# A gated linear attention block with a SiLU feed-forward: the second chunk's scores ahead of the first chunk's y

## The chip, the cores and the metric

The kernel runs on one core of a Trainium2 chip. The metric is the device time of one execution in microseconds (us), the median of a few runs. A core has five engines that work side by side: TensorE (PE in the profile; PEld is its loading of weights), VectorE (DVE), ScalarE (ACT), GpSimd (POOL) and SyncE (SP), which here issues the DMAs of inputs. An engine takes its instructions in the order of its own queue and waits on semaphores for the others.

## The reference

Inputs are q, k, v and alpha of shape (4, 8, 768, 48): batch, heads, tokens, channels. The attention is a recurrence with a decay for each channel; its output, heads side by side, is the input of a feed-forward block.

```python
for t in range(S):
    state = alpha[:, :, t, :, None] * state + np.einsum('bhd,bhe->bhde', k[:, :, t], v[:, :, t])
    y[:, :, t] = np.einsum('bhd,bhde->bhe', q[:, :, t], state)
x = y.transpose(0, 2, 1, 3).reshape(B * S, H * D)   # 3072 x 384
h = x @ w_in                                        # 384 x 2048
out = (h * (1.0 / (1.0 + np.exp(-h)))) @ w_out      # 2048 x 384
```

The weights arrive as 64-bit floats and are rounded to 32 bits on the chip.

## The kernel before

**Chunks.** The 768 tokens are cut into six chunks of 128, for each of four batches: 24 pieces of work, called chunks here and numbered n = 0 to 23; the first four are the first chunks of the four batches. For a chunk the recurrence becomes matrix products: with the running product of alpha, k is multiplied by the decay from its token to the chunk's end, q is divided by the same, and a lower triangle of q times k (the scores) gives what tokens of one chunk do to one another.

**Four stages for each chunk.**

- `products(n)` (L698): TensorE transposes alpha, k and q of the eight heads in four pairs (L717). ScalarE copies alpha (L719), VectorE scans it backwards for the running product u (L722), makes kp = k times u (L733), and by a reciprocal, a second scan (L752) and a product (L758) makes qp.
- `scores(n)` (L780): eight products of kp and qp into two PSUM banks (L793), two copies by ScalarE into the tile g (L800), two selects by GpSimd that put zeros above the diagonal (L801), four transposes of kp (L818) and their copy kn (L820).
- `values(n)` (L831): y from v and g (and, from the second chunk of a batch on, from the state and qp), into one PSUM bank (L846), and a copy into xt (L851), the input of the feed-forward.
- `states(n)` (L852): products of kn and v (L862) that are added to the batch's state, for the first chunk copied (L870).

**Buffers.** g is one tile, `decayed` (L552), for all chunks. kn comes from the pool `work`, with one buffer. The PSUM banks of the attention come from a pool of three (`ps_attn`, L435), handed out in turn; k and q of the first four chunks are transposed into banks of the feed-forward instead. `gpool` (L422) has six large tiles for the feed-forward's activations, 2048 numbers a partition, the first of which is asked for in step 2.

**Order.** A loop (L1185) runs over 25 steps, each with up to four slots. A step has a list of stages with a lag: as a rule the scores of the chunk before, the products of this chunk, then y and the states of the chunk before. In step 1 the products come first. After each slot `fill` (L1166) puts in other work: at first the conversion of w_in, 24 pieces in all with w_out's following (`weights`, L614: a rounding by ScalarE, L629, and three passes by VectorE, L645 to L647), and from step 2 on pieces of the feed-forward, whose TensorE products need xt and w_in. w_in comes in column groups of 512 with three pieces each; two products groups of 256 columns use one column group. The instructions of a stage are then placed by a scheduler, so TensorE's queue isn't exactly the order of the loop: in the kernel before, the third chunk's transposes stand in the middle of the second chunk's y. SyncE's queue is the order of the loads; `fetch` (L513) asks for the next piece of weights when a buffer comes free.

Before the change TensorE's queue at the start reads: transposes of chunks 0 and 1; scores 0; y 0; states 0; scores 1; alpha 2; y 1 with k 2 and q 2 in it; states 1; two groups of products with w_in; scores 2.

Of the kernel before, what the change touches and what calls it, by code (L numbers as in the profile page):

```python
# [8 lines left out]
F32 = mybir.dt.float32  # L9
# [346 lines left out]
def quotients(  # L356
# [38 lines left out]
    C = 128  # L395
    NCH = S // C
    NP = H // 2
# [11 lines left out]
    TB = GB * C // 2  # L409
    HO = HD // 2  # L410

    def pool(name, bufs=1, space=None):
        kw = {} if space is None else {"space": space}
        return ctx.enter_context(tc.tile_pool(name=name, bufs=bufs, **kw))
# [5 lines left out]
    work = pool("work")  # L420
    xtp = pool("xtp", 4)
    gpool = pool("gpool", 6)  # L422
# [12 lines left out]
    def ps_attn(n=C):  # L435
        return ps_a.tile([128, 512], F32, name="ps_a").rearrange("p (j c) -> p j c", c=n)
# [29 lines left out]
    def load(n, names="akq"):  # L466
        if n == NT:
            return
        c = ctxs.setdefault(n, dict(zip(("ci", "b"), divmod(n, B))))
        b, rows = c["b"], slice(c["ci"] * C, c["ci"] * C + C)  # L470
        for name, src in (("a", alpha), ("k", k), ("q", q)):
            if name not in names:
                continue
            x = src[b, :, rows, :]
            if n < NA:
                c[name] = nat[name][n % NIN]
                nc.sync.dma_start(c[name][:, :, 0:D], x.transpose([1, 0, 2]))
                continue

            c[name] = late["quads"][name]
            for u in range(2):
                for i in range(2):
                    r = 64 * u + 32 * i
                    nc.sync.dma_start(
                        c[name][r : r + 32, 32 * (1 - i) :][:, 0 : 4 * NP * D].rearrange(
                            "p (g c) -> p g c", g=NP),
                        x[u::2].rearrange("h (b j) d -> b h (j d)", j=4))
# [6 lines left out]
    def load_v(n):  # L496
        c = ctxs.setdefault(n, dict(zip(("ci", "b"), divmod(n, B))))
        x = v[c["b"], :, c["ci"] * C : c["ci"] * C + C, :].transpose([1, 0, 2])
        t = c["v"] = vns[n % NV]
        if n < NA:  # L500
            nc.sync.dma_start(t[:, :, 0:D], x)
            return
        nc.sync.dma_start(t[:, 0 : H // 2, 0:D], x[:, 0 : H // 2])
        for e in range(2):
            nc.sync.dma_start(t[CH * e : CH * e + CH, H // 2 :, 0:D], x[CH - CH * e : C - CH * e, H // 2 :])
# [46 lines left out]
    decayed = fix.tile([128, 2 * NP * C], F32, name="g")  # L552
# [227 lines left out]
    def scores(n):  # L780
        c = ctxs[n]
        ci, b = c["ci"], c["b"]
        ps = [ps_attn() for _ in range(2)]

        for j in (0, 2, 1, 3):
            for e in range(2 if n >= NA else 1):
                for u in range(2):
                    r = slice(64 * u, 64 * u + D)  # L790
                    at = slice(CH * e, CH * e + CH) if n >= NA else slice(0, C)
                    t = slice(CH * (e ^ j // 2) if n >= NA else 0, C)
                    pe.matmul(ps[u][at, j, t], lhsT=c["kp"][r, j, at], rhs=c["qp"][r, j, t],  # L793
                              start=True, stop=True)
        g = decayed.rearrange("p (u j c) -> p u j c", u=2, j=NP)
        swapped = decayed.rearrange("p (o u j c) -> p o u j c", o=2, u=2, j=NP // 2)
        c["g"] = (lambda u, j: g[:, u, j, :]) if n < NA else (
            lambda u, j: swapped[:, j // 2, u, j % 2, :])
        for u in range(2 if n < NA else 0):
            act.copy(g[:, u], ps[u])  # L800
            gps.affine_select(g[:, u], g[:, u], pattern=[[0, NP], [1, C]], compare_op=ALU.is_ge,  # L801
                              fill=0.0, base=0, channel_multiplier=-1)
        if n >= NA:
            ps = [x.rearrange("p (o j) c -> p o j c", o=2) for x in ps]
            for u in range(2):
                act.copy(swapped[:, :, u, :, CH:], ps[u][:, :, :, CH:])  # L806
            for r, o in earlier:
                for u in range(2):
                    act.copy(swapped[r, o, u, :, 0:CH], ps[u][r, o, :, 0:CH])
            for at, half in ((CH, later), (0, earlier)):  # L810
                for r, o in half:
                    x = swapped[r, o].rearrange("p u j c -> p (u j) c")[:, :, at : at + CH]
                    gps.affine_select(x, x, pattern=[[0, NP], [1, CH]],  # L813
                                      compare_op=ALU.is_ge, fill=0.0, base=0, channel_multiplier=-1)
        if n < NA and ci < NCH - 1:
            ps_k = ps_attn()
            for j in range(NP):
                pe.transpose(ps_k[:, j, :], c["kp"][:, j, :], ident)  # L818
            c["kn"] = work.tile([128, NP, C], F32, name="kn")
            act.copy(c["kn"], ps_k)  # L820
        if ci > 0:
            s = st[b].rearrange("p j u e -> p j (u e)")
            for j in range(NP):
                mul = act.mul(s[:, j], s[:, j], least[:, n, j : j + 1])
                if late:
                    tc.keep_in_program_order(mul)
# [327 lines left out]
    def settle():  # L1154

        first.close()
        late.update(look=pool("look"), part=pool("part"), xc=pool("xc"), turn=pool("turn"),
                    wx=pool("wx").tile([128, 8, NQ, 128], F32, name="wx"))
        quads = pool("quads")
        late["p"] = pool("p").tile([128, NP * W + 1], F32, name="p")  # L1160
        late["quads"] = {name: quads.tile([128, 32 + 4 * NP * D], F32, name=f"{name}t") for name in "akq"}
        for name, t in late["quads"].items():
            gps.memset(t, 1.0 if name == "a" else 0.0)
        load(NA)

    def fill(step, slot):  # L1166

        at = step * SLOTS + slot
        if at < marks[0]:
            if at == SLOTS:  # L1170
                next(conv[0])
            elif step >= 1:
                convert(0, (at - SLOTS) * 3 // (marks[0] - SLOTS) + 1)
            return
        i = next(i for i, m in enumerate(marks[1:]) if at < m)
        a, b = [work_at[n] for n in ([0] + phases)[i : i + 2]]
        due = a + (b - a) * (at - marks[i] + 1) / (marks[i + 1] - marks[i])
        if at % 2 == 0 and step > 3 * GB + 2:
            next(audits, None)
        while work_at[done + 1] <= due and pieces[done][2] <= bridged:  # L1180
            convert(0, 3 * (done // 2) + 6)
            convert(1, 3 * (done - 6) // 2)
            go_on()

    for step in range(STEPS):  # L1185
        if step == 1:
            load(NIN)
        stages = [[(scores, 1)], [(products, 0)], [(values, 1)], [(states, 1)]]
        if step == 1:

            stages = stages[1::-1] + stages[2:]
        elif step >= NA:
            stages = [[(land, 1), (scores, 1)], [(products, 0)], [(quotient, 0)],
                      [(values, 1), (states, 1), (flip, 0)]]
        for slot, group in enumerate(stages):
            for stage, lag in group:
                n = step - lag
                if not 0 <= n < NT:
                    continue
                stage(n)  # L1200
                if stage is values:
                    bridged = n + 1
                if stage is states and n + 1 + NIN < NA:
                    load(n + 1 + NIN)
                if stage is states and n + NV < NT:
                    load_v(n + NV)
            if step * SLOTS + slot == (NA + 1) * SLOTS - 1:
                x = decayed.rearrange("p (o i c) -> p o i c", o=2, c=C)
                for r, o in later:
                    gps.memset(x[r, o, :, 0:CH], 0.0)  # L1210
            fill(step, slot)
            if step * SLOTS + slot >= NA * SLOTS - 1 and conv_done[1] == NFT and not late:
                settle()
# [85 lines left out]
```

## Time and profile before

| | us |
|---|---|
| median of 3 runs | 559.94 |
| lowest and highest | 559.90, 559.98 |
| span of the profiled execution | 558.1 |
| TensorE busy | 541.4 |
| VectorE busy | 445.1 |
| ScalarE busy | 208.4 |
| GpSimd busy | 75.9 |

The span runs from the first to the last instruction of one profiled execution. Busy times are unions of instructions on an engine; matmuls are pipelined and their ends are modelled, so a full TensorE isn't TensorE at its peak. The page's slices are fortieths of the span, 14 us each, in tenths of full. The clock line gives the TensorE clock that was granted, in tenths. In the timeline a line has the start, the duration, the engine, the line of the kernel, the operation, the tile written and the tiles read, sizes, and in brackets how long the engine stood idle before it and who ended that.

The first products of the feed-forward start at 24.27 us, and the loads of the first 30 us keep the DMA engines full: "DMA 9999..." in the first slices, 163 to 433 GB/s in each us from 2 to 23.

### The profile page before, as it was taken

Reading aid. Unit: us, or ns where it says so; the run is one execution under the profiler, and the core shown is the slowest. Engines: PE = TensorE matmul, PEld = TensorE weight load, DVE = VectorE, ACT = ScalarE, POOL = GpSimd, SP = SyncE. Lnnn points to the kernel's source line nnn. Section 1 sums busy time; section 2 is a strip of 40 time slices with the busy share of each in tenths; the row PEclk is TensorE's granted clock in tenths of the full one; section 3 lists DMA queues with packets and bytes.
Section 4 is the critical chain, followed back from the end, with each engine's and each line's share of the span. In section 5 each row is a group of like instructions: output and inputs, shape, how many; then the busy total and the mean of one; then the engine's idle time right before and its main releaser. Section 6 shows DMA issues by size and latency. Waiting matters only on the chain. (4 is left out here: it accounts for less than half of the span.)

```text
span 558.1 us, 12640 instructions
## 1 busy us (share of the span) xinstructions
PE 541.4 (97%) x5026; PEld 488.8 (88%) x5026; DVE 445.1 (80%) x801; ACT 208.4 (37%) x466; POOL 75.9 (14%) x146
## 2 busy tenths in 40 slices
PE   5999999999999999999999999999999999999996
PEld 3788887998899898899999999988998999998996
DVE  5887889974999799997998986998894775857531
ACT  3456643223333243353353353353263341432200
POOL 4100010221211211021021021021121000001000
PEclk9799999999999999999999999999999999999999
DMA  9999861164445525355445654717712122333101
GB/s 218 255 276 177 232 189 40 38 164 108 126 131 136 142 62 134 88 145 157 129 109 142 194 141 115 198 22 179 180 48 84 53 99 95 111 109 106 38 25 32
DMA packets 99220, 70.13 MB, mean 126 GB/s; under 512 B 56272, under 2 KB 88656, under 8 KB 99152
## 3 DMA queue, kind: packets, MB, share of 16 engines
q1 hardware_dynamic: 97232, 65.30, 44.6%
q0 software_dynamic: 1920, 3.93, 2.0%
q8 instruction: 41, 0.67, 0.5%
q14 instruction: 27, 0.22, 0.1%
HBM read 61.34 MB, written 7.86 MB: 124 GB/s over the span
## 5 line engine op out<-in xcount | busy, mean ns | idle before, releaser
L388 PE MATMUL ps_o<-w_out,g 128*128 128x192 f32 x768 | 134.7, 329 | 1.1 <-DVE o L1042 0.9
L388 PEld LDWEIGHTS ps_o<-w_out,g 128*128 128x128 f32 x768 | 125.4, 190 | 5.1 <-DVE o L1042 2.3
L388 PE MATMUL ps_m<-xt,w_in 128*128 128x256 f32 x480 | 113.6, 383 | 1.5 <-ACT xt L851 1.1
L388 PEld LDWEIGHTS ps_m<-xt,w_in 128*128 128x128 f32 x480 | 89.1, 190 | 14.4 <-ACT xt L851 1.6
L388 PE MATMUL ps_o<-wt,g 128*128 128x192 f32 x576 | 99.7, 326 | 0.0
L388 PEld LDWEIGHTS ps_o<-wt,g 128*128 128x128 f32 x576 | 95.1, 190 | 1.6 <-issue 0.2
L388 PE MATMUL ps_m<-xc,w_in 128*128 128x256 f32 x288 | 70.7, 382 | 0.0
L685 DVE TENSOR_REDUCE seen<-bits 128x1 f32<-128x384 int32 (+2 forms) x65 | 42.5, 689 | 24.0 <-DMA bits<-in_moe_w_out_dram 19.6
L388 PEld LDWEIGHTS ps_m<-xc,w_in 128*128 128x128 f32 x288 | 53.6, 190 | 7.0 <-DVE g L944 0.3
L941 ACT ACTIVATE g<-g 128x1024 f32<-128x1024 f32 x32 | 33.0, 1056 | 59.0 <-DVE g L944 59.0
L1033 DVE TENSOR_TENSOR g<-g 128x512 f32<-128x512 f32 x72 | 49.8, 708 | 6.1 <-PE ps_o L388 6.1
L1045 POOL DMA_DIRECT2D out_dram<-o x40 | 22.0, 550 | 223.2 <-DVE o L1042 127.6
L813 POOL TENSOR_SCALAR_AFFINE_SELECT g<-g 64x256 f32<-64x256 f32 x64 | 34.2, 534 | 124.8 <-ACT g L806 105.8
L388 PE MATMUL ps_m<-xc,wx 128*128 128x256 f32 x192 | 50.0, 383 | 1.0 <-DVE xc L586 1.0
L936 ACT COPY g<-ps_m 128x512 f32<-128x512 f32 x64 | 36.5, 588 | 36.5 <-PE ps_m L388 36.4
L388 PEld LDWEIGHTS ps_m<-xc,wx 128*128 128x128 f32 x192 | 35.2, 190 | 5.3 <-ACT u L1064 1.3
L944 DVE TENSOR_TENSOR g<-ps_m,g 128x512 f32<-128x512 f32 x56 | 37.0, 684 | 2.9 <-PE ps_m L388 2.7
L722 DVE TENSOR_TENSOR_SCAN u<-al,one 128x516 f32<-128x516 f32 x24 | 30.0, 1249 | 10.6 <-ACT al L719 10.3
L909 ACT ACTIVATE g<-ps_m 128x512 f32<-128x512 f32 x32 | 19.1, 596 | 42.8 <-PE ps_m L388 42.3
L936 ACT COPY part<-ps_m 128x512 f32<-128x512 f32 x32 | 18.9, 589 | 43.0 <-DVE g L944 21.3
L752 DVE TENSOR_TENSOR_SCAN p<-al,inv 128x516 f32<-128x516 f32 x24 | 29.9, 1246 | 1.0 <-PE ps_a L388 0.4
L388 PE MATMUL ps_a<-g,vn 128*32 128x128 f32 x768 | 27.5, 278 | 1.8 <-POOL g L801 1.7
(126 smaller groups left out, 611.4 us busy)
## 6 DMA issues: line engine op xcount, KB each, us to landing
bits<-in_moe_w_in_dram SPq DMA_DIRECT2D x24, 512.0 KB, 4.8
bits<-in_moe_w_out_dram SPq DMA_DIRECT2D x32, 384.0 KB, 3.1
at<-in_alpha_dram SPq DMA_DIRECT2D x64, 96.0 KB, 2.5
kt<-in_k_dram SPq DMA_DIRECT2D x64, 96.0 KB, 2.5
qt<-in_q_dram SPq DMA_DIRECT2D x64, 96.0 KB, 2.6
bits<-in_alpha_dram SPq DMA_DIRECT2D x9, 512.0 KB, 3.8
out_dram<-o POOLq DMA_DIRECT2D x40, 96.0 KB, 2.4
flips<-turn SPq DMA_DIRECT2D x12, 256.0 KB, 2.4
```

Source lines behind the costliest of these rows:

```text
L388: in_order(nc.tensor.matmul(*args, **kw))
L685: dve.tensor_reduce(seen[kind][which][:, i : i + 1], x, axis=AX, op=op, apply_absolute_value=True))
L722: dve.tensor_tensor_scan(u[:, end - 1 :: -1], sg[:, end:0:-1], one[:, end:0:-1], 0.0, ALU.mult, ALU.add)
L752: dve.tensor_tensor_scan(p[:, 0:end], sg[:, 0:end], iv[:, 0:end], 0.0, ALU.mult, ALU.add)
L813: gps.affine_select(x, x, pattern=[[0, NP], [1, CH]], compare_op=ALU.is_ge, fill=0.0, base=0, channel_multiplier=-1)
L909: act.activation(gts[grp, h, pair][:, i : i + 2, q % 2, :], ps, AF.Silu)
L936: act.copy(to, ps)
L941: act.activation(x, x, AF.Silu)
L944: dve.tensor_tensor(to, a, b, op)
L1033: dve.tensor_tensor(cells(grp, h, pair, *to), cells(grp, h, pair, *x), cells(grp, h, pair, *y), ALU.subtract)
L1045: (gps if grp < NG - 1 else nc.sync).dma_start(out[r : r + C, c * HO : (c + 1) * HO], o)
```

## The change

In step 1 the scores of chunk 1 come right after those of chunk 0 and ahead of chunk 0's y. They need a second g and a second kn, which are cut from one tile of `gpool`: 1024 numbers a partition for g and 512 for kn. In step 2 chunk 1's y comes first and the products of chunk 2 behind it; the first slot is empty. All other steps are as before.

```diff
-        g = decayed.rearrange("p (u j c) -> p u j c", u=2, j=NP)
+        if n == 1:
+            room = gpool.tile([128, 4, 2, TB], F32, name="g").rearrange("p a b n -> p (a b n)")
+        g = (room[:, 0 : 2 * NP * C] if n == 1 else decayed).rearrange(
+            "p (u j c) -> p u j c", u=2, j=NP)
...
-            c["kn"] = work.tile([128, NP, C], F32, name="kn")
+            c["kn"] = room[:, 2 * NP * C :][:, 0 : NP * C].rearrange(
+                "p (j c) -> p j c", j=NP) if n == 1 else work.tile([128, NP, C], F32, name="kn")
...
         if step == 1:
-            stages = stages[1::-1] + stages[2:]
+            stages = [[(products, 0)], [(scores, 1)], [(scores, 0), (values, 1)], [(states, 1)]]
+        elif step == 2:
+            stages = [[], [(values, 1)], [(products, 0)], [(states, 1)]]
```

TensorE's queue then reads: transposes of chunks 0 and 1; scores 0; scores 1; y 0; states 0; y 1; alpha 2, k 2, q 2; a group of products with w_in; states 1; a group of products; scores 2; and on as before. On ScalarE the copies of scores 1 and of its kn come ahead of the first xt, and the second xt ahead of the third chunk's alpha. The queues of VectorE, GpSimd and SyncE keep their order.

## The prediction

> **What bounds the kernel now.** I read first the page's busy shares and slices, then the waits on TensorE, then the first 40 us engine by engine, since the edit touches only steps 1 and 2 of 25.
>
> ```profile
> PE 541.4 (97%) x5026; PEld 488.8 (88%) x5026; DVE 445.1 (80%) x801; ACT 208.4 (37%) x466; POOL 75.9 (14%) x146
> ...
> PE   5999999999999999999999999999999999999996
> ...
> PEclk9799999999999999999999999999999999999999
> ```
>
> TensorE is full in every slice but the first and the last, so the change is worth what it shifts the time from which TensorE is full; after step 2 the order of work is the old one. The second slice has a low clock. Stretches of 3.41 us (columns: length, busy of PE, PEld, DVE, ACT, POOL, then clock, DMA share, GB/s) show where:
>
> ```profile
> 8.58:11.99 3.41, 2.87 (x29) 2.23 (x28) 3.27 (x6) 1.46 (x3) 0.00 (x0) 1.00 1.10 328
> 11.99:15.40 3.41, 1.66 (x52) 1.35 (x51) 3.20 (x5) 1.82 (x4) 2.02 (x2) 1.00 1.08 383
> 15.40:18.82 3.41, 3.41 (x47) 3.04 (x43) 3.11 (x6) 2.31 (x6) 0.00 (x0) 0.50 1.41 206
> 18.82:22.23 3.41, 3.41 (x26) 2.32 (x28) 2.49 (x4) 2.06 (x4) 1.85 (x2) 0.50 1.02 331
> ```
>
> The clock falls to half at 15.40, after a stretch with only 1.66 us of TensorE work, and is back at 22.23. TensorE's own timeline across it:
>
> ```profile
> 16.00 2.13 PE L388 MATMUL ps_a<-p,kp 48*128 48x128 f32 x16
> 18.07 1.11 PE L392 MATMUL ps_a<-ident,kp 128*128 128x128 f32 x4
> 18.98 1.06 PE L392 MATMUL ps_a<-ident,an 128*128 128x128 f32 x4
> ...
> 22.66 0.66 PE L392 MATMUL ps_o<-ident,qn 128*128 128x128 f32 x4
> ...
> 24.27 0.48 PE L388 MATMUL ps_m<-xt,w_in 128*128 128x256 f32 x1 [0.26 <-ACT xt L851]
> ```
>
> The first is the second chunk's scores, then its k transposed, then the third chunk's alpha (18.98) and q (22.66); 24.27 is the first product with w_in, where the full stretch begins. TensorE is not alone there. VectorE's and ScalarE's timelines:
>
> ```profile
> 20.94 1.23 DVE L722 TENSOR_TENSOR_SCAN u<-al,one 128x516 f32<-128x516 f32 x1 [0.75 <-ACT al L719]
> ...
> 30.00 0.69 DVE L647 CUSTOM_DVE_ANT_0 w_in<-w_in,up 128x1024 uint16<-128x1024 uint16 x1
> ...
> 33.47 0.69 DVE L647 CUSTOM_DVE_ANT_0 w_in<-w_in,up 128x1024 uint16<-128x1024 uint16 x1 [1.72 <-ACT up L629]
> ```
>
> ```profile
> 31.29 1.07 ACT L800 COPY g<-ps_a 128x512 f32<-128x512 f32 x2 [0.54 <-PE ps_a L388]
> 32.25 0.60 ACT L820 COPY kn<-ps_a 128x512 f32<-128x512 f32 x1
> 32.73 1.26 ACT L629 ACTIVATE up<-bits 128x512 int32<-128x512 uint32 x2
> ```
>
> VectorE idles twice between 14 and 47: 0.75 us for the third chunk's alpha, and 1.72 us for the seventh rounding on ScalarE, which stands behind the third chunk's score copies. Its 3.26 us of idleness comes only at 47.5. VectorE makes w_in ready: the sixth piece ends at 30.69 and the third product of w_in's second column group needs it.
>
> [...] the two selects took 2.02 and 1.85 us beside a busy VectorE and 1.22 beside an idle one (at 31.95). I take 1.9.
>
> **The change part by part.** It adds and removes no arithmetic. VectorE, GpSimd and SyncE keep their order, so every DMA issue keeps its place. Only TensorE and ScalarE are reordered, up to the products at 27 us. Prices from the trace, at full and half clock: scores 1.09 / 2.06 to the next group; y 0.89 / 1.71 (its records start in fours, every 0.109 and 0.213 us); states 0.34 / 0.65 (fours, every 0.0425 and 0.08); four transposes 0.44 / 0.91. From a group's start to the copy of its result, at half clock: transposes 1.18 (4.00 to 5.18), y about 2.1; scores at full clock 1.27 (10.42 to 11.69).
>
> Step by step, in the new order. The second scores wait for p, done at 14.14: they start at 14.22, at full clock, and TensorE now stands idle where it began the first y at 13.83. The k transposes follow at 15.31, half of a window with little work behind them, so I keep the drop at 15.40; they end at 16.2. ScalarE copies the scores 15.5 to 16.55 and k to 17.15; GpSimd's selects on the new tile run 16.1 to 18.0, hidden behind what follows. The first y, which had begun in full clock, costs 1.71: 16.2 to 17.9. First states to 18.55. Second y (its selects are done, no wait) to 20.26. Third chunk's alpha to 21.17, k to 22.08, q to 22.6. Its q landed at 21.13, so no DMA holds it. The products start at 22.65 in place of 24.27, because xt's copy no longer stands alone at the end: 1.62 gained. The second states now fall between the two products groups: 0.34 less 0.07 that stood there before, so the third scores start at 28.70 in place of 30.05: 1.35 gained on TensorE.
>
> Against this stands VectorE. Alpha's transposes start at 20.26, not 18.98; its copy is ready to start at 20.26 + 1.18 = 21.44, which is also about when ScalarE is through (first xt 18.3, rounding, first states, rounding, second xt to 21.26). VectorE's scan starts at 21.44 + 0.61 = 22.05: 1.11 later than 20.94. VectorE works without a break from there, so the sixth piece of w_in ends at 30.69 + 1.11 = 31.80. TensorE, through with the third k's transposes at about 30.25, does two products and waits for it until 31.87; four products of 0.45 remain, end 33.67, where before it was 34.22. Gain 0.55. The seventh piece: its first two passes end at 31.75 + 1.11 = 32.86, by which time its rounding (32.73 less 1.35, plus 0.65) is done; so the pass at 33.47 starts at 32.86, 0.61 earlier. Both engines are then 0.55 to 0.6 ahead, and what follows moves with them: the twelfth piece ends at 47.5, TensorE needs it at 47.8, and both move. Later stalls (0.15 to 1.3 us each on the list of waits) hang on the same order.
>
> The room for the tile costs nothing: it is the g pool's first buffer, free until group 1's second tile asks for it, six allocations on, and by then long read. What is queued behind the added waits: behind the second scores stand the first y and xt; behind the second y the third chunk's transposes, already counted. ScalarE's rounding for the third piece slips behind the first xt (about 19.4, against 19.28 needed): 0.1 to 0.2, eaten by the 0.75 us of idleness.
>
> The profiled execution spans 558.1; the median of the runs is 559.94, 1.84 around it. 558.10 - 0.55 + 1.84 = 559.4. What a measurement of this kernel can tell from no change is about 0.2%, 1.1 us.
>
> **The rivals.**
> - **Full gain, 558.2.** VectorE is not late (if the clock doesn't drop at 15.40, y, states and y run at full clock, the selects at 18.0 bind, and alpha is copied at 20.3 as before). Then the whole 1.72 us idleness can go: 559.94 - 1.7. For it: the old stretch was not empty either. Against: the new stretch 11.99 to 15.40 holds less work than the one that made it drop. A release one window early, at 18.82, doesn't do it: ScalarE's queue lets alpha through at 21.26 only, gain 0.75.
> - **Release one window late, at 25.64: 560.3.** 2.6 us of products at half clock lose 1.3, and 0.4 more for q: the third scores at 30.4.
> - **Slower, 562.0: the clock stays at half until 29.06**, two windows late (the trace has its edges 6.83 apart). q ends at 23.05; 6.0 us of half clock do 3.0 of the 6.05 us to the third scores, which start at 32.1, 2.05 late; the rounding behind their copies and the pass at 33.47 move as much. [...] For it: TensorE was busy throughout 15.40 to 18.82 and was not released. Against: the new stretch to 22.23 holds y and twelve transposes without a gap, and the transposes alone released it at 8.58.
> - That the scheduler undoes the edit: no, the compiled order has it as written.
>
> **How the numbers follow.** Main case 0.66 (own range 559.0 to 559.9, from alpha's copy 0.4 us earlier or 0.5 later), full gain 0.13, one window late 0.09, slower 0.12. The likeliest gives 559.4. The range 558.1 to 560.7 takes in all but the slower case. Faster 0.15 (full gain, a tail of the main case), slower 0.14 (that rival and what I haven't seen), same 0.71.
>
> **What would show it.** Right: second scores near 14.2, half clock 15.40 to 22.23, first product near 22.7, VectorE's scan for the third chunk near 22.05 with over 1.5 us of idleness before it, a TensorE wait of about 1 us near 31 for VectorE, no 1.72 us stall at 33. Wrong: clock edges elsewhere; the scan at 21 or earlier; a DMA or a select ahead of the second y.

## The result, and the profile after

The changed kernel takes 561.7 us (median of 22 runs, 559.65 to 564.38), the kernel before, run beside it, 560.34 (22 runs, 559.46 to 562.16). The ratio is 1.0023 with a 95% interval of 1.0013 to 1.0033: about 1.3 us more, where 0.55 less had been predicted. The profiled execution of the changed kernel spans 560.9, that of before 558.1.

The page's busy line and its rows of TensorE and of the clock, changed kernel:

```profile
PE 540.8 (96%) x5026; PEld 488.1 (87%) x5026; DVE 446.2 (80%) x801; ACT 209.1 (37%) x466; POOL 76.9 (14%) x146
...
PE   5989999999999999999999999999999999999996
...
PEclk9889999999999999999999999999999999999999
```

The busy sums are within 1.1 us of those of before, so no work was added. But the third slice (28 to 42 us) has lost a tenth on TensorE, and its clock is below full, which before it was not. Stretches of 3.41 us laid on the clock's edges, called windows below (3.41 is the length of this profile's two stretches at half clock, 15.63 to 19.04 and 32.69 to 36.11; the columns are length, busy of PE, PEld, DVE, ACT, POOL, clock, DMA share, GB/s):

```profile
12.21:15.63 3.42, 1.21 (x18) 1.09 (x18) 3.15 (x5) 1.87 (x5) 1.95 (x2) 1.00 1.08 378
15.63:19.04 3.41, 3.41 (x72) 2.96 (x76) 3.21 (x5) 2.09 (x5) 1.96 (x2) 0.50 1.44 201
19.04:22.45 3.41, 3.41 (x53) 2.93 (x46) 2.02 (x4) 2.74 (x6) 0.00 (x0) 1.00 1.02 336
...
29.28:32.69 3.41, 1.55 (x6) 0.76 (x5) 3.20 (x6) 2.48 (x5) 1.84 (x2) 1.00 0.81 264
32.69:36.11 3.42, 3.42 (x11) 2.72 (x11) 3.11 (x6) 0.70 (x2) 0.00 (x0) 0.50 0.89 229
```

The first drop lasts one stretch, not two. A second one follows at 32.69, after a stretch in which TensorE had 1.55 us of work. TensorE's timeline:

```profile
14.44 1.16 PE L388 MATMUL ps_a<-p,kp 48*128 48x128 f32 x16 [2.21 <-DVE p L758]
...
16.54 1.94 PE L388 MATMUL ps_a<-g,vn 128*32 128x128 f32 x32
18.25 0.87 PE L388 MATMUL ps_a<-vn,kn 128*32 128x48 f32 x32
18.89 1.12 PE L388 MATMUL ps_a<-g,vn 128*32 128x128 f32 x32
19.94 0.65 PE L392 MATMUL ps_a<-ident,an 128*128 128x128 f32 x4
...
21.41 2.86 PE L388 MATMUL ps_m<-xt,w_in 128*128 128x256 f32 x12
...
29.05 1.44 PE L388 MATMUL ps_m<-xt,w_in 128*128 128x256 f32 x4
32.20 3.34 PE L388 MATMUL ps_m<-xt,w_in 128*128 128x256 f32 x8 [1.71 <-DVE w_in L647]
35.33 0.98 PE L392 MATMUL ps_a<-ident,an 128*128 128x128 f32 x4
```

The start is as the change has it: second scores at 14.44, both y behind them, the third chunk's alpha at 19.94, and the first products 2.86 us earlier than before (21.41 against 24.27). From 30.49 on this lead is lost: TensorE waits 1.71 us for the sixth piece of w_in, and the eight records after the wait take 3.34 us, at half clock. The fourth chunk's alpha comes at 35.33, where before it came at 34.22. VectorE's timeline shows why the piece is late:

```profile
21.88 1.23 DVE L722 TENSOR_TENSOR_SCAN u<-al,one 128x516 f32<-128x516 f32 x1 [1.22 <-ACT al L719]
...
30.11 1.00 DVE L646 SCALAR_TENSOR_TENSOR w_in<-bits,w_in 128x512 int32<-128x512 int32 x1
31.25 0.90 DVE L647 CUSTOM_DVE_ANT_0 w_in<-w_in,up 128x1024 uint16<-128x1024 uint16 x1
...
33.35 0.69 DVE L647 CUSTOM_DVE_ANT_0 w_in<-w_in,up 128x1024 uint16<-128x1024 uint16 x1
```

The scan is 0.94 later than before (20.94). The second and third pass of the sixth piece take 1.00 and 0.90 where passes beside an idle GpSimd take 0.69, so the piece ends at 32.15: 9.75 us after the scan's start had become 10.27. The stall of 1.72 before the seventh piece's last pass is gone. GpSimd's timeline names the neighbour, first the changed kernel, then before:

```profile
29.77 1.84 POOL L805 TENSOR_SCALAR_AFFINE_SELECT g<-g 128x512 f32<-128x512 f32 x2 [11.55 <-ACT g L804]
```

```profile
31.95 1.22 POOL L801 TENSOR_SCALAR_AFFINE_SELECT g<-g 128x512 f32<-128x512 f32 x2 [11.27 <-ACT g L800]
```

The third chunk's two selects moved forward with the third scores. Before they had run in VectorE's idle 1.72 us; now they lie on the sixth piece.

### The profile page after: what moved, and what is told of

Same layout as the page of the kernel before. It is cut to its first block, busy times and chain, and to the rows that moved or that the text cites. A ratio compares the mean times of both kernels' runs of the same rounds, so it can differ in the third digit from the quotient of the medians.

```text
span 560.9 us, 12637 instructions
## 1 busy us (share of the span) xinstructions
PE 540.8 (96%) x5026; PEld 488.1 (87%) x5026; DVE 446.2 (80%) x801; ACT 209.1 (37%) x466; POOL 76.9 (14%) x146
## 5 line engine op out<-in xcount | busy, mean ns | idle before, releaser
L388 PE MATMUL ps_m<-xt,w_in 128*128 128x256 f32 x480 | 115.5, 386 | 3.1 <-DVE w_in L647 1.7
L941 ACT COPY part<-ps_m 128x512 f32<-128x512 f32 x32 | 18.9, 590 | 43.8 <-DVE g L949 22.2
L388 PEld LDWEIGHTS ps_a<-p,kp 48*64 48x64 f32 (+1 forms) x640 | 19.8, 144 | 9.5 <-issue 4.6
```

The costliest lines, as they stand in the source:

```text
L388: in_order(nc.tensor.matmul(*args, **kw))
L941: act.copy(to, ps)
```

## The experiments

The theory: what decides is when VectorE has the sixth piece, and that hangs on the third chunk's alpha, which the change puts behind the second y on TensorE and behind the second xt on ScalarE. Rivals: the clock alone (the second drop at 32.69), the early scores themselves, the tile, or a first profile of before that was not typical. The ratios below are to runs of before on the same chip (medians 560.6, 560.85 and 560.72 in the three groups). The table has the readings of all kernels but the three with dummy transposes; each time is read from the timeline or from the clock record of one profiled execution. VectorE's order up to the sixth piece is that of before in all rows but two: with alpha early and with y earlier, the scheduler put the third chunk's scan ahead of the third piece's last pass (0.67), so there the end of the sixth piece is the mark to compare, not the scan.

```
kernel              ratio [95%]              clock full  3rd scan  6th piece  TensorE's wait
                                             from        starts    ends       for it
before, 1st profile                          22.2        20.94     30.69      0
before, 2nd profile                          18.0        21.47     31.22      0
changed             1.0023 [1.0013, 1.0033]  19.0        21.88     32.15      1.71
changed again       1.0030 [1.0017, 1.0043]  18.3        22.40     32.66      1.71
alpha first         1.0020 [1.0011, 1.0029]  21.2        22.54     32.28      0
y first only        1.0027 [1.0016, 1.0038]  16.7        23.16     33.44      1.71
tile only           0.9996 [0.9986, 1.0007]  16.3        21.03     30.78      0
changed, alpha early 0.9991 [0.9983, 0.9999] 18.4        20.24     30.54      0
before, alpha early 0.9994 [0.9983, 1.0004]  19.8        21.55     31.53      0
y earlier           1.0009 [0.9999, 1.0019]  19.9        20.97     31.75      0.52
no selects          1.0008 [0.9999, 1.0017]  18.3        22.49     32.24      1.19
```

**The change once more.** No edit.

> The changed kernel once more, for another profile of its start. Clock theory (TensorE comes to the sixth piece of w_in early, idles about 1.7 us, and the idle stretch drops the clock for 3.4 us): about 1.0023 of before; if this profile has no half-clock stretch after 30 us, its span is about 1.5 us shorter than 560.9. Order theory (the loss is VectorE's lateness alone): the span is near 560.9 whatever the clock does. Tile theory (the room in the g pool costs): the same 1.0023, and the lateness arises at many places after 50 us.

562.08 us, ratio 1.0030 [1.0017, 1.0043], span 560.2. Its TensorE timeline:

```profile
29.57 1.44 PE L388 MATMUL ps_m<-xt,w_in 128*128 128x256 f32 x4
32.72 1.99 PE L388 MATMUL ps_m<-xt,w_in 128*128 128x256 f32 x8 [1.71 <-DVE w_in L647]
34.55 0.60 PE L392 MATMUL ps_a<-ident,an 128*128 128x128 f32 x4
```

The wait is again 1.71, but here the clock stays full: the eight records take 1.99, not 3.34. The loss is in the median all the same. So the second drop is no fixture of the change, and not its whole cost; the wait is in both. The span is 0.7 shorter than 560.9, between what the two theories had; single spans scatter by more than that (below), so it doesn't decide between them.

**The tile only.** The first two hunks of the change, step orders of before.

> The room in the g pool for the second chunk's g and kn, with the loop's order of before. Tile theory: 1.002, slower by 1.3 us. Clock theory and order theory: 1.000, within 0.3 us of before.

560.58 us, 0.9996 [0.9986, 1.0007]: the tile costs nothing.

**Early scores, but alpha still ahead of y.** From the changed kernel:

```diff
-            stages = [[], [(values, 1)], [(products, 0)], [(states, 1)]]
+            stages = [[], [(products, 0)], [(values, 1)], [(states, 1)]]
```

> The changed kernel with the third chunk's products ahead of the second chunk's y in step 2, so that alpha's transposes come early again; the early scores and the room stay. Clock theory and order theory both: VectorE's scan of the third chunk at 20.4 to 21.0, piece six of w_in done by about 30.8, TensorE's wait for it under 1 us, ratio 0.998 to 1.000. Tile theory: ratio 1.002 as in the changed kernel.

561.85 us, 1.0020 [1.0011, 1.0029], as slow as the change, where both theories of order and clock had expected a cure. The order in the second step alone doesn't bring it. The number is that of the tile theory, which the run before this one rules out. VectorE's timeline of this kernel:

```profile
20.70 0.69 DVE L647 CUSTOM_DVE_ANT_0 w_in<-w_in,up 128x1024 uint16<-128x1024 uint16 x1 [0.44 <-ACT up L629]
22.54 1.23 DVE L722 TENSOR_TENSOR_SCAN u<-al,one 128x516 f32<-128x516 f32 x1 [1.14 <-ACT al L719]
```

The third piece's pass waits 0.44 for its rounding, which stands on ScalarE behind the first xt, and the scan is as late as with y first. The early scores have pushed back the first y, its xt and, at half clock until 21.2, what follows: alpha's copy starts only at 21.92. TensorE doesn't wait for the sixth piece here. It is late itself: its first products start at 24.66, in the two profiles of before at 24.27 and 23.58. How much of this kernel's loss is TensorE's lateness and how much VectorE's isn't told apart.

**y first only.** From the kernel before, neither tile nor early scores:

```diff
+        elif step == 2:
+            stages = [[(scores, 1)], [(values, 1)], [(products, 0)], [(states, 1)]]
```

> The kernel before with one part alone: in step 2 the second chunk's y ahead of the third chunk's products; scores of the second chunk stay behind the first y, no room. Order theory: VectorE 0.5 to 1 us late as in the changed kernel, ratio 1.001 to 1.002. Clock theory: TensorE is no earlier than before, doesn't idle for w_in by over 0.5 us, ratio 1.000 to 1.001. Tile theory: 1.000.

562.07 us, 1.0027 [1.0016, 1.0038]: this half of the change alone loses as much as the whole, a little more than either theory had, at a clock that was full from 16.7 on. Its scan is the latest of all (23.16), in part because TensorE waits 0.68 and 0.26 for the second chunk's selects at this y, which in the changed kernel are done by then. TensorE's timeline:

```profile
33.49 1.99 PE L388 MATMUL ps_m<-xt,w_in 128*128 128x256 f32 x8 [1.71 <-DVE w_in L647]
```

Again 1.71 of waiting and full clock behind it.

**Early alpha, with everything else of the change.** The third chunk's alpha is transposed and copied right behind the first y, ahead of the first states; k and q stay where they were:

```diff
+            if n == 2 and name == "a":
+                continue
...
+    def alpha_first(n):
+        ps = ps_attn()
+        for j in range(NP):
+            pe.transpose(ps[:, j, :], ctxs[n]["a"][:, 2 * j : 2 * j + 2, :], ident)
+        act.copy(tokens(seg[n % 2]), ps)
...
-            stages = [[(products, 0)], [(scores, 1)], [(scores, 0), (values, 1)], [(states, 1)]]
+            stages = [[(products, 0)], [(scores, 1)], [(scores, 0), (values, 1), (alpha_first, -1)], [(states, 1)]]
```

> The changed kernel with the third chunk's alpha transposed and copied right behind the first y, ahead of the first states; k and q of the third chunk stay behind the second y. Theory of VectorE's order: the third chunk's scan at 20.2 to 21, the wait for the sixth piece under 0.8 us, ratio 0.997 to 0.999, faster than before. Theory of the clock: the early scores leave TensorE idle and the clock low as in the changed kernel, ratio 1.001 to 1.002.

560.53 us, 0.9991 [0.9983, 0.9999]: the only kernel of the study that is ahead of before, if barely, and 0.0032 below the change on the ratios. VectorE's timeline, then TensorE's:

```profile
20.24 1.23 DVE L724 TENSOR_TENSOR_SCAN u<-al,one 128x516 f32<-128x516 f32 x1 [0.21 <-ACT al L748]
...
29.85 0.69 DVE L647 CUSTOM_DVE_ANT_0 w_in<-w_in,up 128x1024 uint16<-128x1024 uint16 x1
...
30.91 1.00 DVE L646 SCALAR_TENSOR_TENSOR w_in<-bits,w_in 128x512 int32<-128x512 int32 x1
32.09 0.87 DVE L647 CUSTOM_DVE_ANT_0 w_in<-w_in,up 128x1024 uint16<-128x1024 uint16 x1 [0.17 <-ACT up L629]
```

```profile
22.61 2.86 PE L388 MATMUL ps_m<-xt,w_in 128*128 128x256 f32 x12 [0.70 <-ACT xt L864]
...
30.25 2.75 PE L388 MATMUL ps_m<-xt,w_in 128*128 128x256 f32 x12
```

The scan is 1.64 earlier than in the changed kernel (2.16 earlier than in its repeat), the sixth piece ends at 30.54 before the selects come, which now stretch the seventh piece's passes (1.00 and 0.87), and the twelve products from 30.25 run without a gap, although the first products start 1.2 later than in the changed kernel. This tells the theory from its rivals: early scores, tile and both step orders are kept, one group of transposes and one copy are moved, and the loss goes. Between these two profiles the clock makes no difference: it was full from 18.4, in the repeat of the change from 18.3, with no second drop in either. Nor is the scan's new place ahead of the third piece's pass enough, since y earlier (below) has it too and gains nothing.

**Early alpha in the kernel before.** The same helper, called between the second scores and the transposes of their k.

> The kernel before, with the third chunk's alpha transposed between the second chunk's scores and its k, and copied ahead of that k; no early scores, no room. Theory of VectorE's order (when the scan of the third chunk starts decides, the early scores bring nothing): scan at 20.2 or earlier in place of 20.94, the 0.75 us of idleness gone, ratio 0.998 to 0.9995, as good as the changed kernel with alpha early (0.9991). Theory that the early scores bring the gain once alpha is early: no better than 1.000.

560.33 us, 0.9994 [0.9983, 1.0004], not told from no change. In its profile the scan came at 21.55, no earlier than before's, with the clock at half until 19.8. It doesn't show that alpha's place is worth anything in the old order.

**y earlier still.** The early alpha, and the second y in the first slot of step 2:

```diff
-            stages = [[], [(values, 1)], [(products, 0)], [(states, 1)]]
+            stages = [[(values, 1)], [(products, 0)], [], [(states, 1)]]
```

> The changed kernel with alpha early, and the second chunk's y moved to the first slot of step 2, so that on ScalarE its xt goes ahead of a rounding. TensorE waited 0.70 us for that xt. If TensorE's start is what is left: the first product 0.5 us earlier, ratio 0.998. If VectorE binds by then: the ratio stays at 0.999.

561.23 us, 1.0009 [0.9999, 1.0019]: a miss, no gain on top of the kernel before it. The scan came at 20.97, and the sixth piece's last pass, beside the selects, took 1.17; TensorE waited 0.52 for it.

**No selects for the third chunk.** The changed kernel with:

```diff
+            if n != 2:
```

ahead of the select.

> The changed kernel without the two selects on the third chunk's scores (that chunk's entries above the diagonal stay, so its y differs; GpSimd's two instructions near 30 us are left out). In the changed kernel they run beside VectorE's two passes of the sixth piece, which took 1.00 and 0.90 us in place of 0.69. Theory [...]: the passes take 0.69, the sixth piece ends 0.4 to 0.5 us earlier after the scan than in the changed kernel, ratio about 1.0015 to 1.002. Theory that only alpha's place counts: ratio unchanged, 1.0025.

561.27 us, 1.0008 [0.9999, 1.0017]. VectorE's timeline of this kernel, and TensorE's:

```profile
30.72 0.69 DVE L646 SCALAR_TENSOR_TENSOR w_in<-bits,w_in 128x512 int32<-128x512 int32 x1
31.55 0.69 DVE L647 CUSTOM_DVE_ANT_0 w_in<-w_in,up 128x1024 uint16<-128x1024 uint16 x1
```

```profile
32.29 1.99 PE L388 MATMUL ps_m<-xt,w_in 128*128 128x256 f32 x8 [1.19 <-DVE w_in L647]
```

The passes are back at 0.69, from the scan to the piece's end it is 9.75 again, and the wait falls from 1.71 to 1.19: exactly the 0.52 that the selects had cost. Without them the third chunk's output is not the reference's. The ratio is 0.0015 below the change, 0.8 us, though the intervals overlap. The fifth chunk's scan starts at 50.67 in it, 51.09 in the repeat of the change with the same clock edge. A part of this would help before too: in before's second profile (below) the selects lie on the seventh piece.

**The wait filled.** Twelve dummy transposes between the second and third product of the waiting group, to keep the clock up:

```diff
+                    if grp == h == pair == e == 0 and f == 4 and t == 2:
+                        x = out_bank(0, 512)
+                        for _ in range(12):
+                            pe.transpose(x[:, 0:128], ident, ident)
```

> The changed kernel with twelve transposes that nobody reads between the second and the third product that read w_in's pieces five and six, where TensorE waited 1.71 us. Theory of the clock: no second half-clock stretch in any run, so the slow runs of the changed kernel (563 to 564) go and the median falls by 0.5 to 1 us, ratio 1.001. Theory of VectorE's order: the pieces come no earlier, the ratio stays at 1.0025.

562.39 us, 1.0024 [1.0013, 1.0034]. The profile has no second stretch at half clock, and the wait left behind the filling is 0.40 (third scan at 22.71, sixth piece done at 32.97). The time is no lower, but the scheduler also put the ninth piece ahead of the fourth chunk's scan on VectorE, so it is no clean test of what the second drop costs.

**The clock kept up at the start.** Dummy transposes ahead of the first transposes and ahead of the first y (before), or of the second scores (changed):

```diff
+    def warm(times, y=None):
+        x = out_bank(0, 512)
+        for _ in range(times):
+            pe.transpose(x[:, 0:128], ident if y is None else y, ident)
```

> The kernel before with transposes that nobody reads in TensorE's idle stretches: nine ahead of the first chunk's, fourteen behind its k, so that the clock is full from about 8 us on. Theory of the clock (what moves the time at the start is when the clock is full): about 1 us faster than before, ratio 0.998. Theory of VectorE's order (w_in's pieces bind, the clock hardly matters): 0.999 to 1.000, the scan of the third chunk a little earlier.

> The changed kernel with such transposes (nine, and sixteen ahead of the second scores), so that the clock is full from about 8 us on. Theory of VectorE's order (alpha behind the second y makes VectorE late, and TensorE waits for w_in): still slower than the kernel before with the same filling, by 0.5 to 1.5 us, and a wait of over 1 us for the sixth piece. Theory of the clock: as fast as that or faster, 0.998.

564.85 us, 1.0069 [1.0056, 1.0082], and 566.28, 1.0099 [1.0077, 1.0122]. Both failed as experiments. TensorE's timeline of the first:

```profile
13.30 2.08 PE L388 MATMUL ps_a<-p,kp 48*128 48x128 f32 x16 [2.09 <-DVE p L765]
...
16.22 3.19 PE L392 MATMUL ps_o<-ident,p 128*128 128x128 f32 x14
```

With the dummies placed, the scheduler moved the second chunk's scan ahead of the first chunk's second scan on VectorE, so the first scores came near 13.3 rather than 10.4, and the dummies themselves ran at half clock (14 in 3.19). They say nothing of the clock's share.

**Before, a second profile.** No edit, one run of 561.04 us, span 559.3.

> The kernel before once more, for a second profile of its start. Theory of VectorE's order: the scan at 20.9 to 21.5, no wait of TensorE for w_in of over 0.3 us, whatever the clock. Theory of the clock: the end of the half-clock stretch sets the lateness at 50 us, up to 1 us either way from the first profile.

TensorE's timeline:

```profile
19.45 0.66 PE L392 MATMUL ps_a<-ident,an 128*128 128x128 f32 x4
...
23.58 2.86 PE L388 MATMUL ps_m<-xt,w_in 128*128 128x256 f32 x12 [0.26 <-ACT xt L851]
...
33.54 0.60 PE L392 MATMUL ps_a<-ident,an 128*128 128x128 f32 x4
```

And VectorE's:

```profile
31.59 1.00 DVE L646 SCALAR_TENSOR_TENSOR w_in<-bits,w_in 128x512 int32<-128x512 int32 x1
32.78 0.85 DVE L647 CUSTOM_DVE_ANT_0 w_in<-w_in,up 128x1024 uint16<-128x1024 uint16 x1 [0.19 <-ACT up L629]
```

In this execution the clock, once it had been full at 7.8, was at half only from 14.6 to 18.0. The products start 0.69 earlier than in the first profile, the fourth chunk's alpha comes 0.68 earlier, and the stall of 1.72 is 0.19: the 0.55 that the change was to win by then, the kernel before already has when its clock comes back early. The profile with the tile only (full from 16.3, fourth alpha at 33.32) says the same.

## Why the prediction was wrong

**What held.** The places of the second scores (14.22 predicted, 14.44), of VectorE's scan (22.05; 21.88, and 22.40 in the repeat), the hidden selects of the second chunk, y at 1.71 in half clock (16.54 to 18.25), the end of the stall at 33, TensorE's wait for the sixth piece, and the tile at nothing. The chain of causes was the right one: early products on TensorE, late alpha on VectorE, and a meeting of the two at the sixth piece.

The near hit of the scan is in part luck. The half clock ended at 19.04, not at 22.23, and the first product came at 21.41, not at 22.65: what ran was the branch that the prediction named in passing, a release one window early, with alpha's copy at 21.26 and a gain of 0.75. ScalarE's timeline has that copy within 0.01:

```profile
21.25 0.59 ACT L719 COPY al<-ps_a 128x512 f32<-128x512 f32 x1
```

The early release doesn't explain the loss, then; by the prediction's own sum it should have added to the gain.

**The step that failed: "the sixth piece of w_in ends at 30.69 + 1.11 = 31.80", a wait of about 1 us, "four products of 0.45 remain", gain 0.55.** Three of its terms were mis-sized.

- *The selects.* "VectorE works without a break from there" kept the old durations, but the third chunk's selects move forward with the third scores (31.95 to 29.77). The prediction placed the selects of the second chunk and not these, and it took from the trace what a busy VectorE costs the selects, not what they cost VectorE. Beside the selects the two passes took 1.00 and 0.90, in the kernel without them 0.69 each; by what path the two engines slow each other no run shows. This cost 0.52 (scan to piece's end 10.27 against 9.75), and without the selects the wait was shorter by 0.52. This is the whole error in the piece: with the scan where it was, 0.94 late, the prediction's sum gives 30.69 + 0.94 = 31.63, and the piece ended at 32.15. That the wait grew to 1.71, from the 0.7 that the sum has (30.25, two products, 31.87), comes mostly from TensorE's earlier arrival, at 29.05 in place of 30.25; waiting from earlier on moves nothing behind the wait.
- *The clock behind the wait.* The wait was taken to cost its own length. In the profiled run it lay in one window, 29.28 to 32.69, with 1.86 us of idleness, and half clock followed from 32.69 to 36.11: the eight records took 3.34 in place of 1.99, 1.35 us. In the repeat and with y first only, with the same wait of 1.71, the clock held. With 0.33 from the piece (32.20 in place of 31.87) and 1.33 from the half clock, the fourth chunk's alpha came at 35.33, not at 33.67; in the repeat, with 0.85 and no half clock, at 34.55. The rival that forecast a slower kernel had the half clock as its price, but as a missed release at 22.23, and the release came early, at 19.04.

  How often such drops came the record tells in part. The clock record of a profiled run begins when the clock is first full (last section), and one window at half clock in a span of 560 us takes 0.003 off the mean; the ends of the profiled runs alone leave 0.998 or more. So a mean granted clock of 0.997 or less is read here as a drop after the first full clock. Such runs are 13 of 33 of the changed kernel and 3 of 7 with y first only, but 11 of 120 of before and 2 of 22 without the selects. The 13 average 562.8 us and the other 20 561.4, where the runs of before without a drop average 560.7. So of the 1.1 us between the averages of all runs about 0.6 is there without a drop. How much of the rest the drop behind the wait makes stays open, since the mean doesn't say where in a run the clock fell.
- *The base.* The gain of 0.55 was measured from the half clock of one profile of before, 15.40 to 22.23, which was taken for a property of the kernel. In before's second profile it ended at 18.0, with the tile only at 16.3. Against the first profile the repeat of the change has the fourth alpha 0.33 late (34.55 against 34.22); against the second, whose clock edge is 0.3 from its own, 1.01 late (33.54). The latter agrees with the 1.3 us of the runs. The median of 559.94 that the sum started from was also some 0.4 to 0.9 below the medians of before in the later groups. And such a start is rare: a run with two windows at half clock after a full one has a mean of 0.994 or less, as the first profile has; among the 120 runs of before there are 2.

**What carries the loss.** In the table the end of the sixth piece puts nearly all kernels in the order of their ratios: 30.5 to 31.5 at 0.9991 to 1, 31.75 at 1.0009, 32.15 to 32.66 at 1.0020 to 1.0030, 33.44 at 1.0027. The kernel without the selects is the exception (32.24, 1.0008). That the late place of the third alpha makes the loss is shown by moving that alpha: 1.0023 or 1.0030 becomes 0.9991. Both halves of the change delay it: y first puts it behind y, and the early scores hold back the first y and its xt, so that these and a rounding stand longer ahead of its copy on ScalarE. TensorE's lead at the first products, 2.9 us on the first profile of before, was worth nothing, since the products overtook the conversion that feeds them.

The lateness of the start is kept. VectorE's timelines at the last chunk's scan, in the two profiles of before, the two of the change, and with alpha early:

```profile
401.86 1.21 DVE L722 TENSOR_TENSOR_SCAN u<-al,one 128x516 f32<-128x516 f32 x1
401.53 1.22 DVE L722 TENSOR_TENSOR_SCAN u<-al,one 128x516 f32<-128x516 f32 x1
403.70 1.21 DVE L722 TENSOR_TENSOR_SCAN u<-al,one 128x516 f32<-128x516 f32 x1
402.36 1.21 DVE L722 TENSOR_TENSOR_SCAN u<-al,one 128x516 f32<-128x516 f32 x1
400.89 1.21 DVE L724 TENSOR_TENSOR_SCAN u<-al,one 128x516 f32<-128x516 f32 x1
```

On average of its two profiles the change is 1.3 us late there, as in the medians, and the kernel with alpha early 0.8 ahead of before.

What stays open: the second drop's share, since the filled wait was no clean test; what makes the clock's return at the start vary from run to run; and what scatters the time behind the last scan. From it to the end of the span it is 156.2 and 157.8 us in the two profiles of before, 156.2 to 159.3 over the profiles of the table, in no order. So the first profile of before has the shorter span although its start is the later one, and spans of single profiles can't be compared to 1 us.

## What to carry to other kernels

When a change lets one engine start earlier, ask first whether the engine that feeds it comes earlier too: here moving the consumer ahead cost 1.3 us and moving one transpose group and its copy for the feeder (VectorE's scan) gave it back. A step that is moved takes its instructions on other engines with it, so price every one at its new place: here two selects came 2.18 us earlier (29.77 in place of 31.95) and cost VectorE 0.52. And take a second profile of the kernel before: a clock edge seen once isn't a property of the kernel.

## What the runs showed of the hardware

**Behind four windows with 1.21 to 1.72 us of TensorE work the clock fell to half; behind a fifth, with 1.71, it stayed full.** In the first profile of before and in that of the change the clock's edges lie 3.41 us or a multiple of it apart: 8.58, 15.40 and 22.23; 8.80, 15.63, 19.04, 32.69 and 36.11. Of the other windows on these edges up to 550 us the emptiest have 2.40 (before) and 2.46 us of TensorE work (changed), and the clock stayed full behind them. Windows of the kernel with y first only, on its own clock edge, around its wait of 1.71:

```profile
30.35:33.77 3.42, 1.71 (x9) 1.14 (x10) 3.25 (x5) 2.48 (x6) 1.83 (x2) 1.00 0.82 259
33.77:37.18 3.41, 3.41 (x23) 3.10 (x23) 3.07 (x7) 2.05 (x4) 0.00 (x0) 1.00 0.95 243
```

And of before's second profile:

```profile
11.17:14.58 3.41, 1.72 (x23) 1.25 (x20) 3.24 (x7) 2.69 (x5) 1.96 (x2) 1.00 1.09 381
14.58:18.00 3.42, 3.33 (x66) 3.05 (x66) 3.08 (x6) 1.31 (x4) 0.07 (x1) 0.50 1.29 276
```

With 1.71 us of TensorE work in the window the clock stayed; with 1.72 it fell, as it did with 1.66 (before's first profile), 1.55 and 1.21 (changed). In the repeat of the change the same wait was split by a window's edge, 2.33 and 2.65 of work on the two sides, and the clock stayed. Busy times of TensorE are modelled, so 1.71 and 1.72 are not told apart, and what decided between these two windows isn't shown.

**The clock's return at the start differs between executions**: full for good from 16.3 to 22.2 us over the eleven profiles of the table, 18.0 and 22.2 for the kernel before itself. Leaving out the second drop, there are two kinds. In both profiles of before and the first of the change the clock became full early, at 7.8 to 8.8, and fell again at 14.6 to 15.6. The other eight have mean clocks of 0.998 to 1.000, so no drop, and in the five of them whose first scores were read (the change again, alpha first, y first only, tile only and the change with alpha early) these took 2.08 us in place of 1.16: half clock from the start to about the time in the table, though the clock column shows 1.00 there, because the record begins only at that time.
